# Loading r and k for 112 partitions and v without its padding, with a sigmoid as ScalarE's first operation

## The chip, the core and the metric

The kernel runs on one core of a Trainium2 chip. The metric is the device time of one execution in microseconds (us). A core has five engines that run at the same time and wait for each other through semaphores: TensorE (PE, matrix products, with the loading of weights shown apart as PEld), VectorE (DVE), ScalarE (ACT), GpSimd (POOL) and SyncE (SP), which here issues nearly all transfers. The transfers themselves are done by 16 DMA engines that all queues share.

## The reference

Two layers follow one another. The first is a linear attention with a decaying state over 768 tokens, for 4 batches of 8 heads of 48 rows; the second is a gated feed-forward layer on the 3072 tokens that come out of it.

```python
for t in range(S):                       # S = 768
    kt, vt, rt = (k[:, :, t], v[:, :, t], r[:, :, t])
    cur = np.einsum('bhd,bhe->bhde', u[None] * kt, vt)
    y[:, :, t] = np.einsum('bhd,bhde->bhe', rt, state + cur)
    state = w[None, :, :, None] * state + np.einsum('bhd,bhe->bhde', kt, vt)
...
h = x @ w_in                             # x: 3072 x 384, w_in: 384 x 2048
sp = np.where(h > 20.0, h, np.log1p(np.exp(np.minimum(h, 20.0))))
g = h * np.tanh(sp)
return (g @ w_out).astype(np.float32)
```

## The kernel before

**Attention.** The 768 tokens of the four batches are worked through in 24 steps (NS), each of 64 tokens of two of the batches. A step needs three tensors. `rk` holds r and k with the head dimension on partitions: two heads of 48 rows lie in partitions 0 to 47 and 64 to 111 (`ROWS`), so that partitions 48 to 63 and 112 to 127 hold only zeros. Each partition has 1024 fp32 numbers, 4 KB. `rkn` (`kn` for the first four steps) holds k and r with tokens on partitions. `v` holds the values with tokens on partitions, eight heads of 48 numbers, each padded to 64, 2 KB a partition. VectorE multiplies `rk` by powers of the decay (`scale`, L606) and, in the first six steps, r by k (`products_rk`, L610); both read partitions 0 to 111 alone. TensorE makes the scores (L358, the one line of all matmuls), VectorE masks them (L730), TensorE multiplies them with `v`, and the outputs are copied to `x` (L950).

**Feed-forward.** Sixteen tiles of the hidden layer run over each batch of 512 tokens: products into `hp`, a copy out (L1222), the gate on ScalarE as sigmoid, arctan and sine (L1030, L1033, L1036), a product on VectorE (`gf`, L1044 in the first batch of tokens) and products into `acc`. The weights arrive as 64-bit floats in 32 blocks of 768 KB (`wraw`, L455) and are turned into 32-bit floats by ScalarE and VectorE (L471 to L481), and later split in two parts (L497, L499).

**ScalarE's tables.** A function needs its table set loaded. The program puts a load ahead of an operation whose function is not in the set that is there. The sigmoid (L1030) and the sine (L1036) have different sets, the arctan needs none of its own, and `AF.Copy` runs under any. The first operation of ScalarE, at L281, copies one column into `early`, which nothing reads; its load is the first load of the program.

**Order.** A planner (`Flow`) runs over all steps with costs and due times before the program is built, and what it writes down is the order in which every engine, and SP's queue, gets its instructions. The costs in the planner (`LAND`, `SHIFT` and the like) are not touched. SP first issues `FIRST` (L520 to L529): rk of steps 0 and 1, a weight block, v of steps 0 and 1, rk of step 2, and so on. For steps 2 and 3 `rk` lies in the tile `first` and v in `vx`, and from step 4 on `start_step` (L560) issues `rk` (L565), `rkn` (L570) and `v` (L574). In `REST` each weight block is issued only when the block before it has landed (`load_rest`, L543). Steps 0 and 1 multiply 64 columns of v at a time (`spread_y`), with the padding filled in by L822; from step 2 on only the first 48 columns of a head are used (`rows_y`, `state_products`).

Of the kernel before, what the change touches and what calls it, by code (L numbers as in the profile page):

```python
# [10 lines left out]
F32 = mybir.dt.float32  # L11
# [5 lines left out]
AF = mybir.ActivationFunctionType  # L17
# [4 lines left out]
B, H, S, D = 4, 8, 768, 48  # L22
NP = H // 2
# [228 lines left out]


@with_exitstack
def rwkv_mish_kernel(ctx, tc, rkT, rkN, vN, wT, w_in, w_out, consts, rkF, vF, wF, uF, outT):
    nc = tc.nc
    const = ctx.enter_context(tc.tile_pool(name="const", bufs=1))
    stage = ctx.enter_context(tc.tile_pool(name="stage", bufs=2))
    main = ctx.enter_context(ExitStack())
    wpool = ctx.enter_context(tc.tile_pool(name="weights", bufs=W_SLOTS))  # L260
    work = main.enter_context(tc.tile_pool(name="work", bufs=2))
# [6 lines left out]
    bias_ln2, early, ones = (small[:, n : n + 1] for n in range(3))  # L268
# [9 lines left out]
    us = cst[:, N_CST : N_CST + 2 * NP].rearrange("d (p q) -> d p q", q=2)  # L278

    nc.vector.memset(bias_ln2, -math.log(2.0))  # L280
    nc.scalar.activation(early, bias_ln2, AF.Copy)  # L281

    states = const.tile([128, B, NP, 64], F32, name="S")
    first = work.tile([128, 2 * 2 * NP * C + 2 * KT * 64], F32, name="first", tag="x")
# [9 lines left out]
    loaded, loads = {}, {}  # L294
# [159 lines left out]
    def load_weight(c):  # L454
        ins = nc.sync.dma_start(raws[c], weights(c))  # L455
        flow.set(f"issued{c}")
        return ins
# [49 lines left out]

    def load_early():

        vx = work.tile([128, 2, 2, NP, 64], F32, name="vx", tag="gh")  # L510
        for s in range(B):
            if s < 2:
                rk = stage.tile([128, 2, 2, NP, CK], F32, name="rk", tag="rk")
                v = stage.tile([128, 2, NP, 64], F32, name="v", tag="v")
            else:
                rk, v = rkx[:, s - 2], vx[:, s - 2]
            if s % 2 == 0:
                kn = stage.tile([128, 2, DM], F32, name="kn", tag="rkn")
            loaded[s] = rk, kn[:, s % 2], v
        for what, s in FIRST:  # L520
            if what == "raw":
                ins = load_weight(s)
            elif what == "rk":
                ins = nc.sync.dma_start(loaded[s][0], rkT[s])
            elif what == "v":
                ins = nc.sync.dma_start(loaded[s][2], vN[s])
            else:
                ins = nc.sync.dma_start(loaded[s][1], rkN[s][:, 0])
            loads[what, s] = ins  # L529

    def load_rest():
        before, name = None, None
        for what, s in REST:
            if name:
                yield name
            if what not in ("raw", "un"):
                yield "out1"
                yield "state1"
            yield from gated(what, s)
            yield sp(what, 1.2 if what == "raw" else 1.0)  # L540
            ins = load_weight(s) if what == "raw" else start_step(s, what)
            if before:
                tc.add_manual_dep(ins.ins, before.ins.name, sync, reason="one weight block under way at a time")  # L543
            behind_fetch(ins, what, s)
            flow.set(f"{what}{s}")
            if what == "raw":
                if s == 2:
                    continue
                before, name = ins, f"raw{s}"
# [10 lines left out]
    def start_step(s, what):  # L560
        if what == "un":
            ins = nc.sync.dma_start(un, consts[:, N_CST + 2 * NP :])
        elif what == "rk":
            rk = stage.tile([128, 2, 2, NP, CK], F32, name="rk", tag="rk")
            ins = nc.sync.dma_start(rk, rkT[s])  # L565
            loaded[s] = [rk, None, None, None]
        elif what == "rkn":
            n = stage.tile([128, 2, DM], F32, name="rkn", tag="rkn")
            a = slice(0, DM + 64 - D if s < N_PE else 2 * DM)
            ins = nc.sync.dma_start(*(t.rearrange("t a d -> t (a d)")[:, a] for t in (n, rkN[s])))  # L570
            loaded[s][1::2] = n.rearrange("t a d -> t (a d)"), n[:, 1]
        else:
            v = stage.tile([128, 2, NP, 64], F32, name="v", tag="v")
            ins = nc.sync.dma_start(v, vN[s])  # L574
            loaded[s][2] = v
        return ins

    def load_step(s):
        yield f"out{s - 2}"
        yield f"state{s - 2}"  # L580
        for what in ("rk", "rkn"):
            yield from gated(what, s)
            yield sp(what, 1 + (what == "rkn" and s >= N_PE))
            behind_fetch(start_step(s, what), what, s)
            flow.set(f"{what}{s}")

    def load_v(s):
        yield f"out{s - 2}"
        yield f"state{s - 2}"
        yield f"rkn{s}"  # L590
        yield from gated("v", s)
        yield sp("v")
        behind_fetch(start_step(s, "v"), "v", s)
        flow.set(f"v{s}")
# [792 lines left out]
    def downs():  # L1387
# [4 lines left out]
        yield from down_last(NC * NF // FB - 1)  # L1392

    load_early()
    for s in range(NS):
        if s < 2:
# [152 lines left out]
                    put("act", mt, o.T, *at)  # L1549


_INS = ["rkT", "rkN", "vN", "wT", "w_in", "w_out", "consts", "rkF", "vF", "wF", "uF"]


def layouts(r, k, v, w, u, moe_w_in, moe_w_out):


    rk = np.stack([r, k]).reshape(2, 2, 2, 2, NP, 2 * NC, CK, D)

    back = rk[..., ::-1, :]  # L1560
    rkT = np.zeros((2 * NC, 2, 128, 2, 2, NP, CK), np.float32)
    for par in range(2):
        for a, x in enumerate((rk[0], back[1])):
            rkT[:, :, ROWS[par], a] = x[:, :, par].transpose(3, 0, 5, 1, 2, 4)
    rkT = rkT.reshape(NS, 128, 2, 2, NP, CK)

    rkN = back[::-1].transpose(5, 1, 2, 6, 0, 4, 3, 7).reshape(NS, 128, 2, DM)

    vN = np.zeros((2 * NC, 2, 2, CK, 2, NP, 64), np.float32)
    vN[..., :D] = v.reshape(2, 2, NP, 2, 2 * NC, CK, D)[..., ::-1, :].transpose(4, 0, 1, 5, 3, 2, 6)  # L1570
    vN = vN.reshape(NS, 128, 2, NP, 64)
    rows = [h * D + d % D for h in range(2) for d in range(64)]
    wT = w.reshape(2, NP, D).transpose(0, 2, 1).reshape(2 * D, NP)[rows]

    row = []
    for k_ in range(KT):
        for par in range(2):
            row += [(2 * k_ + par) * D + e for e in range(D)]
            row += [(6 + par) * D + 16 * k_ + e for e in range(16)]
    w_in = moe_w_in[np.array(row)].reshape(KT, 128, NW, WG * 128).transpose(2, 1, 0, 3).reshape(NW, 128, WE)  # L1580
    w_out = moe_w_out.reshape(NW, WG, 128, DM).transpose(0, 2, 1, 3).reshape(NW, 128, WE)
    w_in, w_out = (np.ascontiguousarray(a).view(np.int64) for a in (w_in, w_out))

    rkF = rk.reshape(2, B, NP, 2, S, D).transpose(3, 5, 4, 0, 1, 2).reshape(2, D, S, 2, B * NP)
    vF = v.reshape(B, NP, 2, S, D).transpose(2, 3, 0, 1, 4).reshape(2, S, B * NP * D)
    wF, uF = (np.tile(a.reshape(NP, 2, D).transpose(1, 2, 0), (1, 1, B)) for a in (w, u))
    consts = np.zeros((128, N_CST + 2 * NP + DM), np.float32)
    for par in range(2):
        consts[ROWS[par], N_CST + par : N_CST + 2 * NP : 2] = u[par * NP : (par + 1) * NP].T
    consts[:, N_CST + 2 * NP :] = u.reshape(2, NP, D).transpose(1, 0, 2).reshape(1, DM)  # L1590
    j = np.arange(128)
    consts[:, :CK] = CK - 1 - j[:, None] % CK < j[None, :CK]
    unit = np.tile(np.eye(CK, dtype=np.float32)[::-1], (2, 1))
    unit = (unit.view(np.uint32) >> 16).astype(np.uint16)
    consts[:, CK:N_CST] = unit.view(np.float32)
    out = dict(
        rkT=rkT, rkN=rkN, vN=vN, wT=wT, w_in=w_in, w_out=w_out, consts=consts, rkF=rkF, vF=vF, wF=wF, uF=uF
    )
    return {n: np.ascontiguousarray(a) for n, a in out.items()}

# [18 lines left out]
```

## Time and profile before

| | |
|---|---|
| median of 3 runs | 481.0 us (480.55 to 481.21) |
| the profiled execution | 483.64 us, span 481.8 us |
| TensorE busy | 470.2 us (98%), 4918 matmuls |
| VectorE busy | 375.7 us (78%) |
| ScalarE busy | 385.4 us (80%), of it 96 table loads |
| DMA | 60.14 MB, mean 125 GB/s |

The profiled execution is one run of the program under the hardware profiler, 2.6 us longer than the median of the unprofiled ones. Its span runs from the first instruction to the last, and 1.8 us of its time lie outside of the span. TensorE's busy time is modelled at the ends of its instructions, so that a full row means a full queue and not that the array runs at its peak. A mean over the whole span hides that the stages differ: the weights arrive in the first 95 us, in which the DMA engines are busiest.

### The profile page before, as it was taken

To read this page: it belongs to the slowest core of one execution; us is meant where nothing else is said; L and a number is where in the kernel's file an instruction comes from. 1 tells how busy PE (TensorE), PEld (TensorE's weight loads), DVE (VectorE), ACT (ScalarE), POOL (GpSimd) and SP (SyncE) were. 2 spreads that over 40 slices of the span, in tenths; PEclk is the share of its full clock that TensorE was granted. 3 is DMA by queue.
4 is the path that set the end of the run, shared out by engine and by line. 5 is a ranking of instruction groups with operands and counts; after the bars stand their busy time and mean duration, and the time that the engine had idled before them with its cause. 6 is when DMAs were issued, how large, how long until landed. Compare 5 with 4: busy or idle time off the path is not lost.

```text
span 481.8 us, 11503 instructions
## 1 busy us (share of the span) xinstructions
PE 470.2 (98%) x4918; PEld 380.6 (79%) x4918; DVE 375.7 (78%) x599; ACT 385.4 (80%) x488; POOL 4.2 (1%) x31
## 2 busy tenths in 40 slices
PE   8989999899999999999999999999999999999996
PEld 5678988566887888888888888888888888888884
DVE  7898897999899975779975789987778754656551
ACT  5669796979999888586889878888579698989971
POOL 1000000000000000000000000000000000000000
PEclk8999999999999999999999999999999999999999
DMA  8866665621424120344142445234453220412001
GB/s 313 289 230 215 208 234 173 229 88 31 160 84 137 39 78 0 101 146 140 69 153 87 166 144 189 80 98 150 163 189 127 66 83 0 132 65 65 2 0 70
DMA packets 20168, 60.14 MB, mean 125 GB/s; under 512 B 3312, under 2 KB 4304, under 8 KB 20112
## 3 DMA queue, kind: packets, MB, share of 16 engines
q1 hardware_dynamic: 17664, 55.11, 34.0%
q10 hardware_dynamic: 2448, 4.25, 2.5%
q8 instruction: 39, 0.64, 0.6%
q14 instruction: 17, 0.14, 0.1%
HBM read 52.57 MB, written 4.72 MB: 119 GB/s over the span
## 4 chain that ended last, share of the span: by engine, by line
PE 70%; DMA 12%; DVE 11%; ACT 4%; SPq 1%; issue 1%; ACTq 0%; DVEq 0%
PE acc L358 33%; PE hp L358 33%; DMA wraw<-in_w_in_dram 5%; DMA wraw<-in_w_out_dram 4%; PE pa L358 3%; DMA kn<-in_rkN_dram 2%; DMA first<-in_rkT_dram 1%; DVE w L499 1%; PE yt L358 1%; DVE wraw L481 1%; DVE gl L1054 1%; DVE hb L1222 1%; DVE hb L1046 1%; SPq L963 1%; DVE rk L606 1%
## 5 line engine op out<-in xcount | busy, mean ns | idle before, releaser
L358 PE MATMUL hp<-x,w 128*128 128x512 f32 x720 | 172.7, 392 | 1.0 <-DVE hb L1222 1.0
L358 PE MATMUL acc<-gh,w 128*128 128x512 f32 x492 | 158.5, 391 | 0.0
L358 PEld LDWEIGHTS hp<-x,w 128*128 128x128 f32 x720 | 134.2, 188 | 29.7 <-DVE hb L1222 1.1
L358 PEld LDWEIGHTS acc<-gh,w 128*128 128x128 f32 x492 | 92.3, 188 | 19.5
L358 PE MATMUL acc<-gl,w 128*128 128x512 f32 x246 | 95.1, 389 | 0.0
L1046 DVE TENSOR_TENSOR hb<-hb,fa 128x1024 f32<-128x1024 f32 x40 | 48.8, 1221 | 37.1 <-ACT fa L1036 37.1
L1030 ACT ACT_TABLE_LOAD x48 | 61.6, 1283 | 13.2 <-DVE hb L1046 9.8
L1036 ACT ACT_TABLE_LOAD x47 | 60.3, 1283 | 0.8
L1222 DVE COPY hb<-hp 128x512 f32<-128x512 f32 x63 | 43.4, 689 | 20.1 <-PE hp L358 19.8
L1030 ACT ACTIVATE fa<-hb,small 128x1024 f32<-128x1024 f32 x48 | 55.3, 1153 | 2.6 <-DVE hb L1046 2.1
L358 PEld LDWEIGHTS acc<-gl,w 128*128 128x128 f32 x246 | 46.2, 188 | 9.5
L1033 ACT ACTIVATE fa<-fa 128x1024 f32<-128x1024 f32 x48 | 50.9, 1060 | 0.8
L1036 ACT ACTIVATE fa<-fa 128x1024 f32<-128x1024 f32 x47 | 49.9, 1061 | 0.5
L1054 DVE TENSOR_TENSOR gl<-hb,gh 128x1024 fp32r<-128x1024 f32 x40 | 48.9, 1222 | 0.6
L358 PE MATMUL acc<-gf,wraw 128*128 128x256 f32 (+1 forms) x132 | 37.8, 439 | 1.6 <-issue 1.6
L358 PEld LDWEIGHTS acc<-gf,wraw 128*128 128x128 f32 x132 | 25.6, 196 | 11.3 <-issue 8.4
L1222 ACT COPY hb<-hp 128x512 f32<-128x512 f32 x33 | 19.3, 584 | 17.2 <-PE hp L358 17.2
L606 DVE TENSOR_TENSOR rk<-rk,TR 112x1024 f32<-112x1024 f32 x22 | 26.9, 1221 | 1.0 <-DMA rk<-in_rkT_dram 1.0
L1050 DVE CAST gh<-hb 128x1024 fp32r<-128x1024 f32 x29 | 20.0, 691 | 7.0 <-PE acc L358 5.5
L471 ACT ACTIVATE wraw<-wraw 128x768 f32<-128x768 uint32 x16 | 14.7, 922 | 11.3 <-DMA wraw<-in_w_out_dram 8.1
L358 PE MATMUL hp<-x,wraw 128*128 128x256 f32 x96 | 22.4, 386 | 0.0
L358 PE MATMUL hp<-xp,w 128*128 128x512 f32 x72 | 18.7, 406 | 2.0 <-ACT w L497 1.3
(143 smaller groups left out, 546.7 us busy)
## 6 DMA issues: line engine op xcount, KB each, us to landing
wraw<-in_w_in_dram SPq DMA_DIRECT2D x16, 768.0 KB, 5.5
wraw<-in_w_out_dram SPq DMA_DIRECT2D x16, 768.0 KB, 4.7
rk<-in_rkT_dram SPq DMA_DIRECT2D x22, 512.0 KB, 4.3
rkn<-in_rkN_dram SPq DMA_DIRECT2D x18, 384.0 KB, 5.4
v<-in_vN_dram SPq DMA_DIRECT2D x22, 256.0 KB, 4.4
out_dram<-ob ACTq DMA_DIRECT2D x10, 256.0 KB, 2.1
x<-x SPq DMA_DIRECT2D x60, 32.0 KB, 2.0
out_dram<-we ACTq DMA_DIRECT2D x6, 256.0 KB, 3.9
```

The source lines that it names most:

```text
L358: ins = nc.tensor.matmul(out, lhsT=lhsT, rhs=rhs, **flags)
L471: nc.scalar.activation(r, low, AF.Copy, bias=2.0, scale=2.0**-51)
L481: v.tensor_tensor(out=up.bitcast(I32), in0=e.bitcast(I32), in1=r.bitcast(I32), op=ALU.add)
L499: nc.vector.tensor_tensor(out=w[:, 1], in0=e, in1=w[:, 0].bitcast(F32), op=ALU.subtract)
L606: nc.vector.tensor_tensor(out=ab, in0=ab, in1=TR[:112].unsqueeze(1).broadcast_to([112, 4, NP, CK]), op=ALU.mult)
L1030: nc.scalar.activation(o.g, o.hb, AF.Sigmoid, bias=bias_ln2, scale=1.0)
L1033: nc.scalar.activation(o.g, o.g, AF.Arctan)
L1036: nc.scalar.activation(o.g, o.g, AF.Sin, scale=2.0)
L1046: nc.vector.tensor_tensor(out=o.hb, in0=o.hb, in1=o.g, op=ALU.mult)
L1050: (nc.scalar.copy if engine == "act" else nc.vector.tensor_copy)(out=o.gh, in_=o.hb)
L1054: nc.vector.tensor_tensor(out=o.gl, in0=o.hb, in1=o.gh.bitcast(F32), op=ALU.subtract)
L1222: (nc.scalar.copy if engine == "act" else nc.vector.tensor_copy)(out=o.hb[:, j], in_=h)
```

## The change

Three things are changed. The transfers of `rk` (L524, L565) load partitions 0 to 111 and leave 112 to 127 as they are. The values come from two arrays: `vN` now holds only steps 0 and 1, padded to 64 as before, and a new array `vD` holds them for every step without padding; from step 2 on v is loaded from it (L526, L574), and its tiles are 48 instead of 64 wide. The function at L281 is a sigmoid instead of a copy.

```diff
-    nc.scalar.activation(early, bias_ln2, AF.Copy)
+    nc.scalar.activation(early, bias_ln2, AF.Sigmoid)
...
-        vx = work.tile([128, 2, 2, NP, 64], F32, name="vx", tag="gh")
+        vx = work.tile([128, 2, 2, NP, D], F32, name="vx", tag="gh")
...
             elif what == "rk":
-                ins = nc.sync.dma_start(loaded[s][0], rkT[s])
+                ins = nc.sync.dma_start(loaded[s][0][:112], rkT[s][:112])
             elif what == "v":
-                ins = nc.sync.dma_start(loaded[s][2], vN[s])
+                ins = nc.sync.dma_start(loaded[s][2], vN[s] if s < 2 else vD[s])
...
             rk = stage.tile([128, 2, 2, NP, CK], F32, name="rk", tag="rk")
-            ins = nc.sync.dma_start(rk, rkT[s])
+            ins = nc.sync.dma_start(rk[:112], rkT[s][:112])
...
-            v = stage.tile([128, 2, NP, 64], F32, name="v", tag="v")
-            ins = nc.sync.dma_start(v, vN[s])
+            v = stage.tile([128, 2, NP, D], F32, name="v", tag="v")
+            ins = nc.sync.dma_start(v, vD[s])
...
+    vN, vD = vN[:2], vN[..., :D]
```

The order of SP's queue at the start of the program, the transfers of `FIRST` (a name with an arrow is a tile and the array it comes from, the numbers are partitions and fp32 numbers in each):

```order
-L524 DMA rk<-in_rkT_dram 128x1024 x2
+L524 DMA rk<-in_rkT_dram 112x1024 x2
 L455 DMA wraw<-in_w_in_dram 128x1536
 L526 DMA v<-in_vN_dram 128x512 x2
-L524 DMA first<-in_rkT_dram 128x1024
+L524 DMA first<-in_rkT_dram 112x1024
 L528 DMA kn<-in_rkN_dram 128x384
 L455 DMA wraw<-in_w_in_dram 128x1536
-L526 DMA vx<-in_vN_dram 128x512
-L524 DMA first<-in_rkT_dram 128x1024
-L526 DMA vx<-in_vN_dram 128x512
```

Nothing moved in the queue: the same transfers stand in the same places, and those of rk are 112 partitions high. The two of `vx` become 384 wide.

ScalarE's instructions at the first gate of the feed-forward layer:

```order
 L914 COPY S<-pb 112x4x48 x2
 L1222 COPY hb<-hp 128x512
-L1030 ACT_TABLE_LOAD
 L1030 ACTIVATE fa<-hb,small 128x1024
 L471 ACTIVATE wraw<-wraw 128x768
```

The first of the 48 table loads at L1030 is gone; the load at L281 stays, and the rows around it keep their order. TensorE, VectorE and GpSimd have the same instructions in the same order as before.

## Rows read from the trace of the kernel before

**Rows 1.** Windows: length, busy us (instructions) of each engine, TensorE's clock, DMA share, GB/s.

```profile
10.00:20.00 10.00, 9.37 (x214) 6.78 (x207) 8.78 (x13) 5.79 (x21) 0.00 (x0) 0.86 1.04 391
...
40.00:50.00 10.00, 10.00 (x185) 8.97 (x179) 8.03 (x12) 9.56 (x17) 0.09 (x1) 1.00 0.68 248
...
80.00:90.00 10.00, 8.04 (x35) 6.22 (x34) 7.70 (x14) 6.48 (x10) 0.00 (x0) 1.00 0.62 235
...
160.00:200.00 40.00, 40.00 (x416) 33.08 (x415) 28.11 (x43) 29.19 (x32) 0.18 (x2) 1.00 0.17 50
```

**Rows 2.** The chain that ended last: start us, us, what.

```profile
3.63 7.22 DMA first<-in_rkT_dram
10.87 7.98 DMA kn<-in_rkN_dram
...
38.40 4.53 DMA wraw<-in_w_out_dram
...
42.99 7.30 DMA wraw<-in_w_in_dram
...
50.31 4.29 DMA wraw<-in_w_out_dram
...
77.88 5.59 DMA wraw<-in_w_out_dram
```

**Rows 3.** VectorE in order of time: start us, us, instruction [idle before it <- releaser].

```profile
5.05 0.69 DVE L610 TENSOR_TENSOR q<-rk 112x512 f32<-112x512 f32 x1 [0.52 <-DMA rk<-in_rkT_dram]
...
16.64 0.69 DVE L610 TENSOR_TENSOR q<-first 112x512 f32<-112x512 f32 x1 [1.01 <-DMA first<-in_rkT_dram]
...
30.80 0.70 DVE L1222 COPY hb<-hp 128x512 f32<-128x512 f32 x1
...
34.85 1.24 DVE L1044 TENSOR_TENSOR gf<-hb,fa 128x1024 f32<-128x1024 f32 x1
```

**Rows 4.** TensorE in order of time, the same columns.

```profile
21.86 0.64 PE L358 MATMUL pa<-cst,q 48*64 48x1 f32 x32 [0.23 <-DVE P L730]
...
27.51 2.86 PE L358 MATMUL hp<-x,wraw 128*128 128x256 f32 x12
...
36.19 2.84 PE L358 MATMUL acc<-gf,wraw 128*128 128x256 f32 x12 [1.55 <-issue]
...
85.36 0.74 PE L358 MATMUL hp<-xp,w 128*128 128x512 f32 x2 [1.33 <-ACT w L497]
86.71 3.92 PE L358 MATMUL hp<-xp,w 128*128 128x512 f32 x16 [0.62 <-DVE w L499]
```

**Rows 5.** DMA issues: out<-in, queue, count, KB of one, median us to landing.

```profile
rk<-in_rkT_dram SPq DMA_DIRECT2D x22, 512.0 KB, 4.3
v<-in_vN_dram SPq DMA_DIRECT2D x22, 256.0 KB, 4.4
```

**Rows 6.** Windows of the first stretch and of one x transfer, columns as in rows 1.

```profile
5.00:7.50 2.50, 2.00 (x37) 1.53 (x40) 2.42 (x3) 1.78 (x8) 0.00 (x0) 1.00 1.01 409
7.50:8.50 1.00, 1.00 (x25) 0.89 (x16) 1.00 (x3) 0.27 (x1) 0.00 (x0) 1.00 1.03 397
...
15.00:16.60 1.60, 1.03 (x28) 0.52 (x25) 0.63 (x2) 0.54 (x2) 0.00 (x0) 1.00 1.07 383
...
106.80:107.20 0.40, 0.40 (x3) 0.30 (x2) 0.40 (x1) 0.38 (x1) 0.00 (x0) 1.00 0.37 82
```

**Rows 7.** Windows inside the chain of weight blocks, columns as in rows 1.

```profile
47.00:50.30 3.30, 3.30 (x166) 2.92 (x164) 3.30 (x5) 2.58 (x3) 0.09 (x1) 1.00 0.21 74
...
81.50:84.00 2.50, 2.50 (x12) 1.95 (x10) 0.76 (x2) 0.51 (x1) 0.00 (x0) 1.00 0.03 7
```

**Rows 8.** ScalarE in order of time around the first gate, columns as in rows 3.

```profile
26.81 1.28 ACT L1030 ACT_TABLE_LOAD   x1
...
34.67 0.59 ACT L1222 COPY hb<-hp 128x512 f32<-128x512 f32 x1 [1.30 <-PE hp L358]
```

**Rows 9.** DMA queues: packets, MB, their time as a share of 16 engines' span.

```profile
q8 instruction: 39, 0.64, 0.6%
```

More of the change, by code (lines that the diff above doesn't have):

```diff
@@ L254, in rwkv_mish_kernel @@
 @with_exitstack
-def rwkv_mish_kernel(ctx, tc, rkT, rkN, vN, wT, w_in, w_out, consts, rkF, vF, wF, uF, outT):
+def rwkv_mish_kernel(ctx, tc, rkT, rkN, vN, vD, wT, w_in, w_out, consts, rkF, vF, wF, uF, outT):
     nc = tc.nc
@@ L1549, in rwkv_mish_kernel @@
                     put("act", mt, o.T, *at)
-_INS = ["rkT", "rkN", "vN", "wT", "w_in", "w_out", "consts", "rkF", "vF", "wF", "uF"]
+_INS = ["rkT", "rkN", "vN", "vD", "wT", "w_in", "w_out", "consts", "rkF", "vF", "wF", "uF"]
 def layouts(r, k, v, w, u, moe_w_in, moe_w_out):
@@ L1596, in layouts @@
     out = dict(
-        rkT=rkT, rkN=rkN, vN=vN, wT=wT, w_in=w_in, w_out=w_out, consts=consts, rkF=rkF, vF=vF, wF=wF, uF=uF
+        rkT=rkT, rkN=rkN, vN=vN, vD=vD, wT=wT, w_in=w_in, w_out=w_out, consts=consts, rkF=rkF, vF=vF, wF=wF, uF=uF
     )
```

## The prediction

> **What bounds the kernel now.** The windows by stage come first. From 160 us on TensorE is busy in all of its 40 us, and in all ten of 40 to 50, as in the three windows of ten behind it; holes show at 10 to 20 (0.63 us) and at 80 to 90 (1.96 us) [rows 1]. Transfers that end earlier beside a full TensorE win nothing, so the change can only win in front of a hole. TensorE's own timeline names the holes that matter: 0.23 us at 21.86, 1.55 us ahead of 36.19, and 1.33 and 0.62 us at 85.36 and 86.71 [rows 4]. The chain that ended last says what stands behind them [rows 2]. Up to 18.85 us it is the first transfers, which all wait in one backlog. From 38.40 to 83.47 it is eight weight blocks in a row, each issued when the one ahead has landed; the first, second, third and last of them are shown. Between the two stretches, and for a while behind the second, the chain runs mostly on VectorE and ScalarE. VectorE's timeline shows the link: at 16.64 it has waited 1.01 us for rk of step 3, and then it works without a pause until the product `gf` at 34.85 to 36.09 [rows 3], for which TensorE's hole ahead of 36.19 ends.
>
> The sum is made against the profiled execution, 483.64 us with a span of 481.8. The unprofiled median is 481.0 us, 2.6 us less; what is won lies inside of the span, so I take the same difference off the median.
>
> **Bytes.** An rk transfer has 512 KB [rows 5]; without 16 of 128 partitions it has 64 KB less. At the 409 GB/s of the saturated stretch [rows 6], 65,536 bytes are 0.160 us of 1.28. A v transfer has 256 KB, 0.660 us at the 397 GB/s of the window in which rows of 2 KB run; 192 KB in rows of 1.5 KB are 0.513 us at the 383 GB/s of the window 15.00 to 16.60, in which mostly `kn` runs, whose rows have that size [rows 6]. That saves 0.147 us. There are 24 rk transfers and 22 of v with the short rows, 7.1 us in sum, but 16 of each come after step 7, when the chain no longer stands on a transfer. They are costed at nothing, under a full TensorE; if that cover were gone, at 16 x 0.307 = 4.9 us.
>
> For the 0.160 us the 112 rows must spread over the 16 DMA engines as evenly as 128, seven to an engine instead of eight. No transfer of the trace has 112 rows. From below the price is -0.160 us. From above it is bounded by the transfers of x, 16 partitions of 2 KB from one part of the memory to another: in their window 82 GB/s come at a DMA share of 0.37, 13.9 GB/s for each busy engine, against 409 / (1.01 x 16) = 25.3 for full-height loads [rows 6]. Rows that meet like that would take 1.8 times as long: 1.12 x 1.8 = 2.05 us for an rk transfer, 0.77 us more than now. I take -0.160, because a load of 112 rows of 4 KB from device memory is nearest to the load of 128 such rows; the other end stays as a rival.
>
> **The start, up to 38 us.** Ahead of rk of step 3 in the queue stand three rk transfers and v of step 2, and its own rows end it: 4 x 0.160 + 0.147 = 0.79 us earlier. The wait of 1.01 us at 16.64 [rows 3] can shrink by that or vanish, if an engine that came late in this transfer is met by less backlog. VectorE then starts its unbroken stretch 0.8 to 1.0 us earlier, but TensorE is nearly as full. The copy at 30.80 takes the product that ended at 27.51 + 2.86 = 30.37 us [rows 3, 4]: 0.43 us of slack. TensorE itself loses only the 0.23 us at 21.86. So `gf`, and with it 36.19 and the start of the weight chain, come 0.66 us earlier. Bounds: nothing, if rk lands as late as now, and 0.82 us, if the first wait (0.52 us for rk of step 0 at 5.05, [rows 3]) also shrinks by 0.16. I take **-0.66 us**.
>
> **The weight chain, 38.40 to 83.47.** Between its blocks stand rk of steps 5 to 7 and v of steps 5 to 7: 3 x (0.160 + 0.147) = 0.92 us of transfer time. All of it would count if the DMA engines were the limit, none if these transfers lie in the time between a block's last bytes and the first of the next. Both are seen: the window 47.00 to 50.30 has a DMA share of 0.21 and 81.50 to 84.00 one of 0.03 [rows 7], so that at the end of a block one or two late engines are waited for, and a late engine does have the extra rows ahead of its share of the block. No row decides; I take the middle, **-0.46 us**. What was won in the start carries over, since the chain's first block is issued behind the copies that end the VectorE stretch. At 84 the hole of 1.95 us [rows 4] has room for the 0.46. Behind it VectorE, ScalarE and TensorE all run full and shift together.
>
> **The table load.** The load at 26.81 us (1.28 us) goes. ScalarE is then done earlier, but its next wait is 1.30 us for TensorE's `hp` ahead of 34.67 [rows 8], which grows by what is won, and `gf` at 34.85 starts without idle time on VectorE, after VectorE's own work. So it is worth nothing. If that cover were gone, the 1.28 us would count. It costs nothing either: a load at L281 is there before and after.
>
> **Matmuls with v.** Operands lie 48 instead of 64 apart, with the same shapes and counts; no row shows a price for a stride, and I take none.
>
> The sum is -0.66 - 0.46 = -1.12 us, 482.5 us for a profiled execution and **479.9 us** for the median, 0.23% faster.
>
> **Rivals.** *A, the forecast:* 479.2 to 480.6 us, chance 0.42. Against it speaks that both terms are taken inside wide bounds, for it that the two waits are plainly on transfers.
>
> *B, rk gets no shorter.* If some of the 16 engines, or what they write through, still has eight rows, a transfer of 112 rows ends with the slowest. Then the start wins the 0.147 us of v alone and the chain half of 3 x 0.147 = 0.22: 0.37 us, 480.6 us. Nothing in the trace excludes it, since no transfer there has that height. Chance 0.22. [...]
>
> *C, rk gets longer, and the kernel slower.* The place is the startup. If an engine gets seven neighbouring rows, several engines may write through the same path at a time, as in the x transfers. Each rk transfer that lasts x us longer puts four times x ahead of VectorE's wait at 16.64, less the 0.147 of v, and a longer wait there passes in full to `gf` and to 36.19. From x = 0.04 us on the start is later than now. At x = 0.3, two fifths of the way to the bound of 0.77, the start loses 1.2 - 0.15 = 1.05 us and the chain, by half, 0.5 x 3 x (0.3 - 0.147) = 0.23: +1.3 us, 482.3 us. Against it speaks the saturated stretch, where full-height loads reach 25.3 GB/s per engine. Chance 0.19.
>
> *D, the late engines fall elsewhere.* 39 fetches of instructions took 0.6% of 16 engines' span [rows 9], 0.006 x 16 x 481.8 / 39 = 1.2 us each on one engine. A block whose rows stand behind one is late: 7.30 us against 4.29 for the next [rows 2]. When the start moves by a microsecond, fetches meet other rows. One such block less wins what is left of the hole, some 1.5 us beyond the forecast: 478.4 us; one more, at 7.30 less the 4.53 of a good block, costs 2.8 us: 482.7 us. Chance 0.17, 0.10 of it for the gain.
>
> That the change doesn't do what it says can be left out for the loads: the queue's order shows 112 rows and 384 columns. It is true of the sigmoid in a sense, since its saving is hidden.
>
> **How the numbers follow.** 0.2%, 0.96 us, is about what a measurement of this kernel can tell from no change: below 480.04 is faster, above 481.96 slower. A gives 0.27 faster and 0.15 within; B 0.03, 0.17 and 0.02 slower; C 0.06 within and 0.13 slower; D 0.10, 0.01 and 0.06. Faster 0.40, the same 0.39, slower 0.21. The time is that of A, the likeliest. The range of 478.8 to 482.4 us leaves out the far halves of D and of C, some 0.18 in all; A alone has 479.2 to 480.6.
>
> **What would show it.** Right: VectorE's wait for `first` at L610 is under 0.3 us, `gf` starts near 34.2 us, rk's median landing falls below 4.3 us, the chain of weight blocks takes about 44.6 us, ScalarE has 47 table loads at L1030 and waits longer for `hp` behind the first sine. B: that wait is 0.8 to 1.0 us. C: it is above 1.2 us, and rk's landings are later than now. D: one block of the chain lasts 2 us more or less than it does now, while the others stay. The prediction is wrong at its root if the holes at 36 and 85 us change by an amount that neither wait explains.

## The result: slower by 0.65%, most of it lost in the first 38 us

| | before | after |
|---|---|---|
| median of 6 runs each | 480.63 us (480.22 to 481.21) | 483.73 us (483.15 to 484.58) |
| ratio | | 1.0065, interval 1.0052 to 1.0078 |
| the profiled execution | 483.64 us, span 481.8 us | 483.15 us, span 481.4 us |
| TensorE busy | 470.2 us | 469.3 us |

The spans of the two profiles mislead: they say that nothing happened. The profiled execution of before is an unusually long one of its kernel; three more profiles of before, below, took 480.53, 480.57 and 481.59 us. So places are compared here, not spans.

VectorE after, in order of time (start us, us, instruction [idle before it <- releaser]):

```profile
5.58 0.69 DVE L610 TENSOR_TENSOR q<-rk 112x512 f32<-112x512 f32 x1 [1.04 <-DMA rk<-in_rkT_dram]
...
18.66 0.69 DVE L610 TENSOR_TENSOR q<-first 112x512 f32<-112x512 f32 x1 [1.81 <-DMA first<-in_rkT_dram]
...
36.85 1.23 DVE L1044 TENSOR_TENSOR gf<-hb,fa 128x1024 f32<-128x1024 f32 x1
```

The same three instructions stand in [rows 3] at 5.05, 16.64 and 34.85. The first is 0.53 us late, the second 2.02, and `gf` 2.00: from rk of step 3 on, the delay is passed on whole. TensorE's product behind `gf` moves with it, from 36.19 [rows 4]:

```profile
38.17 2.84 PE L358 MATMUL acc<-gf,wraw 128*128 128x256 f32 x12 [1.54 <-issue]
```

Why rk is late is seen in windows of the first 20 us, after (columns as in [rows 1]):

```profile
5.00:7.50 2.50, 1.05 (x8) 0.97 (x8) 1.88 (x3) 1.71 (x8) 0.00 (x0) 0.96 1.00 274
7.50:10.00 2.50, 2.41 (x39) 2.30 (x39) 2.50 (x5) 1.06 (x3) 0.00 (x0) 0.50 1.07 388
10.00:12.00 2.00, 1.76 (x28) 1.16 (x33) 1.40 (x4) 1.51 (x8) 0.00 (x0) 0.50 1.04 237
12.00:15.00 3.00, 2.67 (x73) 2.13 (x67) 2.86 (x5) 1.31 (x6) 0.00 (x0) 0.65 1.03 375
15.00:18.00 3.00, 2.48 (x75) 1.51 (x75) 1.81 (x3) 1.48 (x3) 0.00 (x0) 1.00 1.02 260
18.00:20.00 2.00, 1.53 (x58) 1.41 (x57) 1.34 (x2) 0.59 (x3) 0.00 (x0) 1.00 1.07 403
```

And of before, whose window 5.00 to 7.50 (409 GB/s) is in [rows 6]:

```profile
7.50:10.00 2.50, 2.33 (x52) 1.73 (x46) 2.50 (x6) 1.74 (x6) 0.00 (x0) 0.89 1.04 409
10.00:12.00 2.00, 2.00 (x69) 1.73 (x62) 1.82 (x4) 1.59 (x7) 0.00 (x0) 0.50 1.07 426
12.00:15.00 3.00, 3.00 (x57) 1.52 (x56) 2.97 (x5) 1.27 (x3) 0.00 (x0) 0.85 1.00 389
15.00:18.00 3.00, 2.37 (x83) 1.79 (x81) 1.99 (x4) 0.94 (x4) 0.00 (x0) 1.00 1.07 402
```

The last two columns are the DMA share and the GB/s. The share is 1.00 to 1.07 everywhere: on the mean, all 16 engines have work all the time. The rate is near 400 GB/s in every window of before, but after falls to 274, 237 and 260 in three of them, in the order in which rk of step 1, rk of step 2 and rk of step 3 pass; between them, in the weight blocks, it is 375 to 403. (Which transfer passes in a window is an estimate from the queue's order and the bytes moved until then; no view times the bytes of one transfer.) The engines are as busy, at a share of 1.00 to 1.04 in these three, and move less. The bytes missing in the five windows, (409 - 274) x 2.5 + (409 - 388) x 2.5 + (426 - 237) x 2 + (389 - 375) x 3 + (402 - 260) x 3 = 1236 KB, take 3.1 us at 400 GB/s; the 4 x 65.5 + 65.5 KB that the change saves ahead of rk of step 3 give 0.8 back. That makes 2.3 us, against the 2.0 seen.

The rest is as forecast or without effect. ScalarE lost its table load, and its wait grew from the 1.30 us of [rows 8]:

```profile
36.67 0.59 ACT L1222 COPY hb<-hp 128x512 f32<-128x512 f32 x1 [2.58 <-PE hp L358]
```

The landings (count, KB, median us), with 4.3 and 4.4 us in [rows 5], moved little, since the medians are made mostly of transfers behind the start:

```profile
rk<-in_rkT_dram SPq DMA_DIRECT2D x22, 448.0 KB, 4.5
...
v<-in_vD_dram SPq DMA_DIRECT2D x20, 192.0 KB, 4.2
```

The chain that ended last begins as in [rows 2], with a first transfer 1.90 us longer than the 7.22 us there; none of its later weight blocks is among its 55 longest pieces now:

```profile
3.59 9.12 DMA first<-in_rkT_dram
12.73 7.79 DMA kn<-in_rkN_dram
```

### The profile page after: what moved, and what is told of

Its sections match the earlier page's. It is cut to its first block, busy times and chain, and to the rows that moved or that the text cites. A ratio compares the mean times of both kernels' runs of the same rounds, so it can differ in the third digit from the quotient of the medians.

```text
span 481.4 us, 11499 instructions
## 1 busy us (share of the span) xinstructions
PE 469.3 (97%) x4915; PEld 381.9 (79%) x4918; DVE 375.7 (78%) x599; ACT 384.8 (80%) x487; POOL 4.6 (1%) x31
## 4 chain that ended last, share of the span: by engine, by line
PE 90%; DVE 4%; DMA 4%; issue 1%; SPq 1%; ACT 0%; POOL 0%; DVEq 0%; POOLq 0%
PE hp L358 42%; PE acc L358 41%; PE pa L358 4%; PE yt L358 2%; DMA first<-in_rkT_dram 2%; DMA kn<-in_rkN_dram 2%; DVE w L499 1%; DVE hb L1222 1%; DVE rk L606 1%; DVE gl L1054 0%; DVE hb L1046 0%; DVE P L730 0%; DVE wraw L481 0%; DVE kn L684 0%; DVE rkn L651 0%
## 5 line engine op out<-in xcount | busy, mean ns | idle before, releaser
L1030 ACT ACTIVATE fa<-hb,small 128x1024 f32<-128x1024 f32 x48 | 55.4, 1153 | 2.6 <-DVE hb L1046 2.1
L471 ACT ACTIVATE wraw<-wraw 128x768 f32<-128x768 uint32 x16 | 14.9, 930 | 7.8 <-DMA wraw<-in_w_out_dram 4.4
L358 PEld LDWEIGHTS hp<-x,wraw 128*128 128x128 f32 x96 | 18.4, 196 | 2.0
```

What stands on the lines that cost most here:

```text
L358: ins = nc.tensor.matmul(out, lhsT=lhsT, rhs=rhs, **flags)
L471: nc.scalar.activation(r, low, AF.Copy, bias=2.0, scale=2.0**-51)
L1030: nc.scalar.activation(o.g, o.hb, AF.Sigmoid, bias=bias_ln2, scale=1.0)
```

## The experiments

**e1: transfers of several heights, alone and eight in a row.** A kernel of transfers only.

```python
def load(t, n, at=0, first=0, step=1, src=rows, alone=True):
    last = first + (n - 1) * step + 1
    ins = nc.sync.dma_start(t[at : at + n], src[first:last:step, : t.shape[1]])
    if alone:
        for p in before:
            tc.add_manual_dep(ins.ins, p.ins.name, sync, reason="one transfer at a time")
...
for w, n in (("full", 128), ("cut", 112), ("six", 96)):
    for i in range(8):
...
        load(tiles[w, i], n, first=128 * i, alone=not i)
```

> This kernel leaves out the whole computation: it writes zeros and loads 4 KB rows of rk (and 1.5 KB rows of v) into tiles of 128, 120, 112, 96 and 64 partitions, one transfer at a time, four times each, and then eight in a row of 128, 112 and 96. Theory P (the rows of a transfer that is not 128 high meet on shared paths into the core's memory): a load of 112 rows lands no earlier than one of 128, although it has 12% less; eight in a row take 8 x 1.28 = 10.2 us at 128 rows and 13 to 15 us at 112; starting at partition 16 or with another row pitch in device memory changes nothing. Theory H (the slow side is device memory, whose addresses are now 28 KB apart from engine to engine): with a pitch of 8 KB a row the load of 112 rows takes another time than with 4 KB. Theory F (112 rows are fine, and it is instruction fetches that came late in the changed kernel): 112 rows land 0.16 us earlier than 128, and eight in a row take 9.0 us.

Median landings of transfers that run alone, and of the last of eight in a row (the names with `many`):

```profile
full<-in_rkT_dram SPq DMA_DIRECT2D x4, 512.0 KB, 3.4
...
odd<-in_rkT_dram SPq DMA_DIRECT2D x4, 480.0 KB, 4.0
cut<-in_rkT_dram SPq DMA_DIRECT2D x4, 448.0 KB, 3.3
...
manyfullh<-in_rkT_dram SPq DMA_DIRECT2D x2, 512.0 KB, 9.7
...
manycuth<-in_rkT_dram SPq DMA_DIRECT2D x2, 448.0 KB, 11.7
```

Alone, 112 rows land about as soon as 128: the medians of four differ by 0.1 us, and one of the four of 128 rows, the first, takes 4.9 us. As the last of eight in a row they land 2.0 us later, with an eighth fewer bytes. So for 112 rows the price, 2.0 us at the eighth, belongs to a backlog here, and a transfer timed alone doesn't show it. Not every height is free alone: 120 rows (`odd`) land at 4.0 us. From its first issue to that of the next group, a row of eight takes 13.6 and 13.5 us with 128 rows and 15.6 and 14.9 with 112; theory P had the order right and the times, 10.2 and 13 to 15, too short, and theory F's 9.0 us for 112 rows falls.

**e2: the kernel before once more**, with no edit, because its first profile was so long.

> The kernel before, unchanged, for a second profile. Theory 1 (the hole of 1.95 us at 85 us belongs to that one execution, which took 483.64 us where six others took 480.2 to 481.2): the time is 480.2 to 481.3, the hole is under 0.5 us, and the wait of VectorE for rk of step 3 at 16.6 us is 0.8 to 1.2 us as before. Theory 2 (the hole is a fixed part of the kernel, which the change took away): the hole is 1.5 to 2.3 us again.

It took 481.59 us. VectorE and, in the second fence, TensorE:

```profile
16.71 0.69 DVE L610 TENSOR_TENSOR q<-first 112x512 f32<-112x512 f32 x1 [0.51 <-DMA first<-in_rkT_dram]
...
34.93 1.21 DVE L1044 TENSOR_TENSOR gf<-hb,fa 128x1024 f32<-128x1024 f32 x1
```

```profile
49.30 0.64 PE L358 MATMUL pa<-cst,q 48*64 48x1 f32 x32 [0.78 <-DVE P L730]
```

`gf` is where it was, and the holes at 85 us in [rows 4] are gone: they belong to that one execution, not to the kernel. This one has a hole of 0.78 us at 49 us instead, its only one between 38 and 140 us; another, of 0.8 to 1.0 us near 148 us, stands in every profile of before and of after. Two figures of the expectation were missed: the time is 0.3 us above its range, and the wait for rk of step 3 is 0.51 us, not 0.8 to 1.2. That wait differs from one execution to the next.

**e3: only the 112 rows.**

```diff
-                ins = nc.sync.dma_start(loaded[s][0], rkT[s])
+                ins = nc.sync.dma_start(loaded[s][0][:112], rkT[s][:112])
...
-            ins = nc.sync.dma_start(rk, rkT[s])
+            ins = nc.sync.dma_start(rk[:112], rkT[s][:112])
```

> The 112 rows of rk alone; v and the first operation of ScalarE as before. Theory P (each rk load of 112 rows takes some 0.5 us longer): VectorE's wait at L610 for rk of step 3 ends near 18.7 us as in the changed kernel, 2 us later than before, and the time is 483.3 to 484.8 us. Rival V (the 1.5 KB rows of v cost it): 480.2 to 481.0 us. Rival S (the sigmoid's place costs it): likewise 480.2 to 481.0.

483.39 us (5 runs, 483.16 to 483.76) against 480.68; ratio 1.0050, interval 1.0032 to 1.0067. VectorE:

```profile
18.99 0.69 DVE L610 TENSOR_TENSOR q<-first 112x512 f32<-112x512 f32 x1 [1.94 <-DMA first<-in_rkT_dram]
```

The height alone makes the loss.

**e4: only the narrow v and the sigmoid**, with rk back at 128 rows.

```diff
-                ins = nc.sync.dma_start(loaded[s][0][:112], rkT[s][:112])
+                ins = nc.sync.dma_start(loaded[s][0], rkT[s])
...
-            ins = nc.sync.dma_start(rk[:112], rkT[s][:112])
+            ins = nc.sync.dma_start(rk, rkT[s])
```

The diff is against the kernel after.

> The changed kernel with rk loaded for 128 partitions again; v without padding from step 2 on and the sigmoid stay. Theory P: 479.9 to 480.7 us, since v of step 2 frees 0.15 us ahead of VectorE's wait and little else can be won. Rivals V or S (v's short rows or the sigmoid cost it): 482.5 to 484 us. If the forecast's terms for v were right in size: 480.3 us.

481.01 us (10 runs, 480.0 to 482.09) against 480.68; ratio 0.9999, interval 0.9986 to 1.0013 (the two medians alone would give 1.0007). The median is 0.3 us above the range of theory P and far below that of V and S. In its profile rk of step 3 is used 0.4 to 0.5 us earlier than in [rows 3] and e2, and `gf` comes as much earlier:

```profile
16.25 0.69 DVE L610 TENSOR_TENSOR q<-first 112x512 f32<-112x512 f32 x1 [0.84 <-DMA first<-in_rkT_dram]
...
34.45 1.21 DVE L1044 TENSOR_TENSOR gf<-hb,fa 128x1024 f32<-128x1024 f32 x1
```

But ScalarE then meets a weight block that isn't there:

```profile
38.59 0.96 ACT L471 ACTIVATE wraw<-wraw 128x768 f32<-128x768 uint32 x1 [3.46 <-DMA wraw<-in_w_out_dram]
```

So a lead at 34 us was met by a wait at 38 us in this execution. The two parts are worth nothing that 10 runs can tell.

**e5: the start's queue, and eight in a row of equal bytes.** Transfers only again, each group begun when the one ahead has landed, and all of it twice: the first eleven transfers of the start with rk of 128 and of 112 rows; eight of 128 rows x 4 KB, 128 x 3.5 KB, 112 x 4 KB and 64 x 4 KB; and eight from device memory to device memory, of 128 and of 112 rows of 1000 numbers.

```python
START = (
    (rows, 1024), (rows, 1024), (blocks, 1536), (values, 512), (values, 512), (rows, 1024), (keys, 384),
    (blocks, 1536), (values, 512), (rows, 1024), (values, 512),
)
...
    ("full", 128, 1024, pool), ("narrow", 128, 896, pool), ("cut", 112, 1024, pool), ("half", 64, 1024, pool),
```

> The whole computation is left out; zeros are written, and groups of transfers are issued without waits inside a group, each group twice. One group is the queue of the kernel's start up to v of step 3 (eleven transfers, rk at 128 or at 112 rows); the others are eight transfers in a row of 128 x 4 KB, 128 x 3.5 KB, 112 x 4 KB, 64 x 4 KB, and from device memory to device memory of 128 and 112 rows of 4000 bytes. Theory P (rows of a transfer that is not 128 high meet on shared paths into the core's memory): in the start's queue the rk of step 3 lands 1 to 2 us later with 112 rows than with 128; the eight of 128 x 3.5 KB, which have the same bytes as the 112 rows, take 7/8 of the 128 x 4 KB, less than the 112 rows by 2.5 us or more; the 64 rows take nearly as long as the 128; between device memory and itself 112 rows take 7/8 of the time of 128. Theory H (device memory is the slow side): there too 112 rows take longer than 128. Theory E (a transfer costs by its engines' rows alone): 112 x 4 KB and 128 x 3.5 KB take the same.

Windows over the first turn of these four, in that order, and then of the two groups from memory to memory (the last two columns are again the DMA share and the GB/s):

```profile
51.14:64.50 13.36, 0.00 (x0) 0.00 (x0) 1.00 0.81 314
64.62:77.00 12.38, 0.00 (x0) 0.00 (x0) 1.00 0.79 296
77.10:93.00 15.90, 0.00 (x0) 0.00 (x0) 1.00 0.85 231
93.00:105.40 12.40, 0.00 (x0) 0.00 (x0) 1.00 0.81 170
105.50:121.40 15.90, 0.00 (x0) 0.00 (x0) 1.00 0.78 258
121.50:135.80 14.30, 0.00 (x0) 0.00 (x0) 1.00 0.74 251
```

The same bytes take 12.4 us as 128 narrow rows and 15.9 us as 112 rows (16.6 in the second turn); 128 whole rows, with more bytes, take 13.4. So it isn't the bytes. An estimate from these windows, share x 16 engines x length / rows, gives the engine time of one row: 0.17 us with 128 rows of 4 KB, 0.24 with 112 and 0.31 with 64, but 0.19 with either height from memory to memory. By this estimate a row itself takes longer, so that idle engines, or one with too many rows, don't explain it alone. Landing of the eighth, and of rk of step 3 in the start's queue (`j`):

```profile
startfullj<-in_rkT_dram SPq DMA_DIRECT2D x2, 512.0 KB, 9.3
...
eightdramfullh<-in_rkT_dram SPq DMA_DIRECT2D x2, 500.0 KB, 10.8
...
startcutj<-in_rkT_dram SPq DMA_DIRECT2D x2, 448.0 KB, 12.5
...
eightdramcuth<-in_rkT_dram SPq DMA_DIRECT2D x2, 437.5 KB, 9.0
```

From memory to memory 112 rows are faster than 128, 1.8 us at the eighth, and are read at 251 GB/s there, above the 231 of the load: reading 112 rows cost nothing extra in this group. The extra time appears only in the loads into partitions, 15.9 us against 13.4. In the start's queue rk of step 3 lands 3.2 us later after its issue, and the group is 1.7 and 2.5 us longer in the two turns (16.5 to 18.2, 15.6 to 18.1): 0.4 to 0.6 us for each of its four rk transfers by the length of the group, 0.8 by that landing. Theory P had expected it 1 to 2 us later; its other signs came out, though the factor of 7/8 did not (12.4 of 13.4 us is 0.93), and theories H and E fell.

**e6: 112 rows only from step 4 on**, the rest as after, and against it the diff.

```diff
-                ins = nc.sync.dma_start(loaded[s][0][:112], rkT[s][:112])
+                ins = nc.sync.dma_start(loaded[s][0], rkT[s])
```

> The changed kernel with rk of steps 0 to 3 loaded for 128 partitions again, later ones for 112. Theory P-start (all of the loss is in the first 20 us): 480.0 to 481.2 us, and VectorE's wait for rk of step 3 ends at 16.2 to 16.8 us. Theory P-all (the weight chain and the later stages lose too): 481.5 to 483 us.

481.33 us (10 runs, 480.33 to 482.85) against 480.85; ratio 1.0005, interval 0.9989 to 1.0022. Twenty transfers of 112 rows, 16 of them under a full TensorE, cost nothing that can be measured; the interval leaves room for 1.1 us, and the median lies between the ranges of the two theories. Its profile, an execution of 482.15 us, has rk of step 3 in time, used at 15.99 us without a wait, and yet a `gf` that is 1.0 us later than in [rows 3]:

```profile
21.05 1.03 DVE L684 TENSOR_TENSOR kn<-kn,TKn 128x384 f32<-128x384 f32 x2 [1.50 <-ACT TKn L351]
...
35.92 1.22 DVE L1044 TENSOR_TENSOR gf<-hb,fa 128x1024 f32<-128x1024 f32 x1
```

So rk of step 3 is not the only thing that can hold VectorE up in the start; the table `TKn` from ScalarE is another.

**e7: 112 rows only in steps 0 to 3**, the rest as before, and against it the diff.

```diff
-                ins = nc.sync.dma_start(loaded[s][0], rkT[s])
+                ins = nc.sync.dma_start(loaded[s][0][:112], rkT[s][:112])
```

> The kernel before with rk of steps 0 to 3 alone loaded for 112 partitions. Theory P-start: 482.8 to 484.2 us, as with all rk loads so. Theory P-all: 481.2 to 482.5 us.

483.93 us (4 runs, 482.64 to 485.1) against 480.85; ratio 1.0062, interval 1.0037 to 1.0086. VectorE:

```profile
18.69 0.69 DVE L610 TENSOR_TENSOR q<-first 112x512 f32<-112x512 f32 x1 [1.87 <-DMA first<-in_rkT_dram]
...
36.90 1.22 DVE L1044 TENSOR_TENSOR gf<-hb,fa 128x1024 f32<-128x1024 f32 x1
```

Four transfers of 24 make the whole loss, at the place and of the size of the kernel after.

**e8: is an earlier rk of step 3 worth anything?** e4, with a weight block and rk of step 3 issued ahead of `kn` and v of step 2; the engines' order is unchanged.

```diff
+ISSUED = [FIRST[n] for n in (0, 1, 2, 3, 4, 5, 7, 9, 6, 8, 10, 11, 12, 13)]
...
-        for what, s in FIRST:
+        for what, s in ISSUED:
```

> rk at 128 rows everywhere, v without padding from step 2 on, the sigmoid first, and in SP's queue alone the second weight block and rk of step 3 are issued ahead of kn and v of step 2; every engine's order stays. It takes away VectorE's wait for rk of step 3 by another means than the forecast's. If that wait is worth what the forecast said: VectorE does not wait at L610, gf starts 0.5 to 0.8 us earlier than in the kernel before, and the time is 479.7 to 480.2 us. Rival (an earlier start is given back later, by the weight chain or by TensorE): the wait goes, gf starts earlier, and the time is 480.3 to 481.3 us.

480.89 us (10 runs, 479.9 to 482.21) against 480.85; ratio 1.0004, interval 0.9994 to 1.0015. VectorE no longer waits for rk of step 3, but:

```profile
20.22 1.03 DVE L684 TENSOR_TENSOR kn<-kn,TKn 128x384 f32<-128x384 f32 x2 [0.82 <-ACT TKn L351]
...
35.10 1.22 DVE L1044 TENSOR_TENSOR gf<-hb,fa 128x1024 f32<-128x1024 f32 x1
```

`TKn` is next in line, and `gf` is no earlier than in [rows 3]. Both expectations had it earlier; the time is in the rival's range. This is also the version that would have beaten both kernels if the start's wait were worth something; it doesn't.

**e9 and e10: before twice more; e11 and e12: after twice more**, no edits. They ask whether the delay of `gf` accounts for the time.

> The kernel before, unchanged, another profiled execution. The two profiled so far took 483.64 us (holes of 1.95 us at 85 us) and 481.59 us (a hole of 0.78 us at 49 us), both with gf at 34.85 to 34.93 us, while the median is 480.7. Theory S (everything the change costs is passed on from gf): gf stands again within 0.2 us of 34.9 us, and an execution of 480.4 to 480.9 us has no hole on TensorE between 40 and 150 us. Theory L (the first 40 us themselves vary): an execution of 480.4 to 480.9 us has gf at about 34.0 us.

> The same kernel and the same numbers once more, because the time of a single execution spreads over 2 us: S, gf at 34.7 to 35.1 us whatever the time, and each hole between 40 and 150 us adds its own length to 480.7 us; L, gf moves by as much as the time does.

> The changed kernel, unchanged, another profiled execution; the first took 483.15 us with gf at 36.85 us and no hole between 40 and 150 us. S: gf stands within 0.2 us of 36.85 us, and the time is 480.7 + 2.0 + whatever holes there are behind 40 us, so 482.7 us if there is none. L: gf differs from 36.85 us by as much as the time differs from 483.15 us.

> The changed kernel once more: S, gf at 36.65 to 37.05 us and a time of 482.7 us plus its holes behind 40 us; L, gf between 36 and 38 us with the time moving along with it.

| execution | us | `gf` starts | TensorE busy in 40 to 100 us |
|---|---|---|---|
| before, e9 | 480.57 | 34.88 | 60.00 |
| before, e10 | 480.53 | 34.97 | 60.00 |
| before, e2 | 481.59 | 34.93 | 59.22 |
| before, first profile | 483.64 | 34.85 | 58.04 |
| after, first profile | 483.15 | 36.85 | 60.00 |
| after, e11 | 483.51 | 37.53 | 59.99 |
| after, e12 | 484.82 | 37.97 | 59.99 |

The use of rk of step 3 in the two later executions of after:

```profile
19.33 0.69 DVE L610 TENSOR_TENSOR q<-first 112x512 f32<-112x512 f32 x1 [1.45 <-DMA first<-in_rkT_dram]
```

```profile
18.88 0.69 DVE L610 TENSOR_TENSOR q<-first 112x512 f32<-112x512 f32 x1 [1.31 <-DMA first<-in_rkT_dram]
```

One more execution of before, run beside these and without a profile, took 482.89 us; none of after is under 483.15. Four executions of before have `gf` within 0.12 us, and what they differ in comes behind it. The three of after are 1.9, 2.6 and 3.0 us late at `gf` and 2.6, 3.0 and 4.3 us late at the end, against e9 and e10. On the mean that is 2.5 of 3.3 us, measured from the two fastest executions of before. The expectation that `gf` stays within 0.2 us of 36.85 after fell; that the time follows `gf` held, to 0.4 to 1.2 us, and that last part I could not trace to one place; the first profile of before has such a rest too, 1.1 us beyond the 1.96 that TensorE lacks in 40 to 100 us.

In e9 `gf` isn't released by rk of step 3 at all; VectorE waits for `TKn`, and `gf` is where it is in e10, which waits for rk:

```profile
20.01 1.03 DVE L684 TENSOR_TENSOR kn<-kn,TKn 128x384 f32<-128x384 f32 x2 [0.86 <-ACT TKn L351]
```

```profile
16.77 0.69 DVE L610 TENSOR_TENSOR q<-first 112x512 f32<-112x512 f32 x1 [1.24 <-DMA first<-in_rkT_dram]
```

In e12 a second loss joins the first. TensorE waits 1.22 us ahead of 18.84 us and is busy for 1.16 of the two us around it; then its granted clock, 1.00 until there, falls:

```profile
18.00:20.00 2.00, 1.16 (x50) 1.09 (x51) 1.12 (x2) 0.22 (x2) 0.00 (x0) 1.00 1.09 391
20.00:22.00 2.00, 2.00 (x18) 1.61 (x13) 2.00 (x3) 2.00 (x8) 0.00 (x0) 0.63 1.02 412
22.00:24.00 2.00, 2.00 (x7) 1.57 (x6) 2.00 (x5) 1.25 (x3) 0.00 (x0) 0.52 0.48 190
```

It is 0.63 on the mean of 20 to 22 us and 0.52 of 22 to 24, and the first product for `hp` takes 4.55 us where the next takes 2.87. In after's first profile the clock is 1.00 in these windows. `gf` is 19.09 us behind the use of rk of step 3 (18.88) in e12, and 18.19 in the first profile: 0.9 us on top. The lower clock alone doesn't make this loss: in e11 the granted clock is 0.50 from 20 to 22 us and the first product for `hp` takes 4.55 us too, but it starts at 19.33, as rk of step 3 is used, and `gf` follows that use by 18.20 us. In e12 the product starts 1.56 us behind the use (1.41 in the first profile, at a clock of 1.00), and VectorE later waits for TensorE. TensorE in e12, then that wait:

```profile
18.84 0.34 PE L358 MATMUL pa<-cst,q 48*64 48x1 f32 x10 [1.22 <-issue]
...
20.44 4.55 PE L358 MATMUL hp<-x,wraw 128*128 128x256 f32 x12
...
26.73 2.87 PE L358 MATMUL hp<-x,wraw 128*128 128x256 f32 x12
```

```profile
31.05 0.29 DVE L950 COPY x<-hp 128x128 f32<-128x128 f32 x1 [0.74 <-PE yt L358]
```

## Why the prediction was wrong

**The price of an rk transfer: the step that failed.** The prediction took -0.160 us and gave the range of -0.160 to +0.77. The windows of after give, at 274 GB/s in the window that holds rk of step 1, 458,752 bytes / 274 = 1.67 us against 1.28, so +0.39 us; e5 gives +0.4 to +0.8 in the start's queue, and eight in a row +0.2 to +0.4 a transfer (e1, e5). The bound from the x transfers pointed the right way, and I set it aside because a load of 112 rows looked like a load of 128. That is a likeness of size and source, and the price shows only in the loads into partitions (e5: 15.9 us against 13.4, where from memory to memory it is 14.35 against 16.1), for which the x transfers were the one row that spoke. e1 shows how easily it could have been missed: alone, 112 rows land no later than 128.

**Rival C was what happened**, with its place, its chain of waits and its sign: the wait for rk of step 3 is above 1.2 us in all profiles of after (1.81, 1.45, 1.31), and the delay passes in full to `gf` and to TensorE's product behind it. The length of the wait is a poor sign, since e10 has 1.24 us in the kernel before; the time of the use is a good one, 15.59 to 16.77 us in four profiles of before and 18.66 to 19.33 in three of after. The reason that C gave, several engines on one path, was not shown: no view has a path, or the rows that an engine gets. It put x at 0.3 us; with 0.4 to 0.6 its own formula, 4x - 0.147, gives 1.5 to 2.25 us, and 1.9 to 3.0 were seen. It had a chance of 0.19, and its 482.3 us was short of 483.73 by this size and by what e12 and the untraced part add.

**Rival B fell**: rk got longer, not equal. Eight loads of 112 rows took 15.9 us against 13.4 for eight of 128 (e5), and rk of step 3 was used at 18.66 to 19.33 us in three profiles of after, against 15.59 to 16.77 in four of before. Its premise, that some engine or path still has eight rows, was not shown: how rows are dealt to engines is in no view.

**The start, -0.66 us: wrong beyond its price.** With the wait removed (e8) `gf` came no earlier, since `TKn` is ready only just before; e9 shows the same in the kernel before. Where `TKn` was in time (e4), `gf` came 0.4 us earlier, and the kernel was no faster. A wait of 1.01 us in one execution was taken for slack that could be won, without asking what is next in line on the same engine.

**The weight chain, -0.46 us: wrong.** It needed the hole at 85 us. Two of four executions of before have a full TensorE from 40 to 100 us, and there is nothing to win there; that [rows 4] came from an execution 2.6 us longer than the median was in front of me. The reading of one or two late engines was loose as well: shares of 0.21 and 0.03 are 3.4 and 0.5 of 16 engines on the mean.

**Right:** the table load is worth nothing (its 1.28 us went into the wait of 2.58; the trace of before has 97 table loads in all, not the 96 of the table of times), the 16 later transfers of each kind are hidden (e6), and narrow v has no price and no measurable gain (e4). Rival D isn't needed for the loss: e7 gives it again, at the same place, with only four transfers changed.

## What to carry to other kernels

Cutting padding partitions off a load saves bytes and can still cost time: with an eighth of the bytes gone, eight loads took 15.9 us instead of 13.4 (e5), and the kernel 483.39 us instead of 480.68 (e3). Where such loads run in a backlog that something waits for, try them 128 partitions high and cut the length of the rows instead, which was timed here in transfers alone (12.4 against 13.4 us, e5). Time such a shape in a row of its like (9.7 and 11.7 us at the eighth, e1), not alone (3.4 and 3.3). Before a wait is priced as a gain, look for the next releaser on the same engine, and take holes only from executions near the median.

## What the runs showed of the hardware

Eight loads in a row took 13.4 us with 128 rows of 4 KB, 12.4 with 128 rows of 3.5 KB, and 15.9 and 16.6 with 112 rows of 4 KB in e5, 15.6 and 14.9 in e1; 96 rows took 14.0 in e1, and 64 rows 12.4, at half the bytes of 128. The engines' busy share is alike (0.79 to 0.85 in e5) while the rate goes from 170 to 314 GB/s; in the kernel's windows 5.00 to 7.50, 274 GB/s stand beside a share of 1.00 (after) and 409 beside 1.01 (before). So a busy share of 1 didn't mean here that the transfer rate was at its top. From memory to memory 112 rows took 14.35 and 128 rows 16.1 in the first turn. The engine time of a row, estimated in e5, is 0.17, 0.24 and 0.31 us for 128, 112 and 64 rows on the way into partitions; in e1, slices in which the engines were busy for 90% or more moved 374 and 362 GB/s with 128 rows, 270 to 291 with 112 and 267 to 272 with 96, which at a share of 0.95 to 1 is an estimate of 0.17 to 0.18 us for 128 and 0.21 to 0.25 for 112 and for 96. From memory to memory it doesn't rise (0.19 at either height, e5). Why a row takes longer is not shown: how rows are dealt to engines, and whether they share a path into the partitions, is in no view here.
